# Gated layer: when the rooms in U's place are given out, and where the output's weights load

## The chip, the cores and the metric

The kernel runs on one core of one Trainium2 chip. The metric is the device time in microseconds (us) of one execution. The engines are called as in the profile: PE is TensorE (matmuls; PEld its weight loads), DVE is VectorE, ACT is ScalarE, POOL is GpSimd, and SP is SyncE, which here issues all DMAs. Each engine executes its own instructions strictly in the order of the program.

## The reference, cut to what matters

Three layers follow one another: attention over 8 heads with a window of 128 positions, a feed-forward layer with relu, and the gated layer, which the change is about. Batch is 4, sequence 576, model width 512.

```
def _moe2_ref(x, w_in, g_ln, w_sg, b_sg, w_out):        # x: 4 x 576 x 512
    h = gelu(x @ w_in)                                  # w_in: 512 x 1024
    u, v = h[..., :512], h[..., 512:]
    v_n = (v - mean(v)) / sqrt(var(v) + 1e-6) * g_ln    # over the last dimension
    v_s = einsum('ts,bsd->btd', w_sg, v_n) + b_sg       # w_sg: 576 x 576
    return x + (u * v_s) @ w_out                        # w_out: 512 x 512
```

All of it is computed in f32 quality. On the PE every f32 operand is split into a high and a low part (suffix h and l), and each product takes three matmuls: high x high, high x low, low x high. The high part is written by ScalarE (L1149), the low part is the difference to the source, written by VectorE or GpSimd (L1152).

## The kernel before, in words

**An order made by a planner.** The program is not written in a fixed order. Generators yield `Op`s, each with an engine, an expected duration, a priority, the tokens it needs and the buffers it takes. The class `Sched` (L115 to L208) simulates the engines, always takes the operation that can start earliest (among equal starts the one with the lower priority number), and lets its generator emit the instructions. So the planner's own estimates decide the order of the instructions on every engine. On the chip only that order and the semaphores count. For a load (an Op with a size, L197 to L199) it assumes 1100 ns until the transfer starts, 300 bytes per ns one transfer after another, and 1600 ns until its readers may start. Operations of the gated layer have priorities from 1000 up, except V's and U's weights and batch 0's x, which have 940 to 980.

**The gated layer** is `Phase2` (from L985). Its units of work run on the PE in this order (L992 to L994): V of batch 0, U of batch 0, Vt (V of the last 64 tokens of all four batches, taken together), V and U of batches 1, 2, 3, Ut (U of those last tokens), then S of batch 0 and 1 (the spatial product of w_sg and v), O 0 and 1 (the output of two groups of 256 tokens), S 2, O 2, O 3, S 3, O 4 to O 8. Each of V, U and S works on four quadrants with seven products of blocks instead of eight (`CHAIN`, L979), and so needs seven blocks of each operand: some are quadrants, some sums or differences of quadrants. Blocks of x are called bX, of the normalised v bN, of gated values bG. The seven products of a unit go to three PSUM banks. Product 1 is evicted by ScalarE (`evac`, L1397, into a tile te) before the third product of the chain may use its bank again; sums are made by VectorE (L1403), then GELU by ScalarE (L1420), or for S the gate (L1603, L1610).

**Rooms.** SBUF of the gated layer is handed out as numbered rooms of a kind ("X", "V", "Y", "te", "tt"). A room's entry carries the token that says from when the planner thinks it free. Rooms of kind V hold u, v, the three blocks of the last tokens' x, and gated blocks. The blocks of batch 1's and 3's v go to rooms of kind Y: three rooms of the pool p2c, and six that are cut out of the place of U's weights (tiles "more", L1375 to L1382). Those six are given out when the planner emits the fourth kind of product (P == 4, the chain's last) of U of batch 3. The tile framework makes the first write to a "more" tile wait on the chip for every matmul that still reads U's weights. Ut, which comes next on the PE, reads them too (L1501). `prep_v(1)` (L1273) begins the blocks of batch 1's v when that same product of U is done.

**Loads.** The weights of the output (wo: four pieces of 512 KB, `f64`, L1118) may load once `open_4` has run at the end of the feed-forward layer (token "room", "late"). There are two staging tiles (st), so two of them load at once and the third follows when the first piece has been worked on: ScalarE takes an absolute value (L84), VectorE does four bit operations (L89 to L96), then the split follows. The last tokens' x is loaded by `load_tail` (L1279), batch 1's x by `load_x` (L1258) in two loads; the planner plans the latter at the end of the first product of U of batch 0, and SP issues them in that order without waiting for it. All of them go through SP's one queue.

Of the kernel before, what the change touches and what calls it, by code (L numbers as in the profile page):

```python
# [8 lines left out]
F32R = mybir.dt.float32r  # L9
# [9 lines left out]
B, H, S, D = 4, 8, 576, 64  # L19
# [16 lines left out]
HOP, HOPD, HOPP = 160, 127, 280  # L36
# [78 lines left out]
class Sched:  # L115
# [49 lines left out]
    def run(self, until):  # L165
        while until not in self.done:
            best = None
            for n, p in enumerate(self.procs):
                t = self.ready(p)
                if t is None:  # L170
                    continue
                op = p[2]
                if op.alt:
                    op.eng, op.dur = min(op.alt, key=lambda z: self.at(z[0], t, z[3:]) + sum(z[1:3]))[:2]
                    op.port = op.eng == "DVE" and len(max(op.alt, key=len)) > 3
                start = self.at(op.eng, t, op.port) if op.eng else t
                key = (start + TRADE * min(max(op.pri, -99), 99), op.pri, n)
                if best is None or key < best[0]:
                    best = key, p
            assert best, [(p[2].eng, p[2].token, [x for x in p[2].need if x not in self.done], p[2].slots)  # L180
                          for p in self.procs][:40]
            (_, _, _), p = best
            op = p[2]
            t = self.ready(p)
            start = self.at(op.eng, t, op.port) if op.eng else t
            for name, bufs, tok in op.slots:
                self.slots[name].append(tok)
            for kind, n, tok in op.take:
                for _, z in self.free_of(kind)[:n]:
                    self.stock[kind][z][2] = tok  # L190
                    op.got.append(self.stock[kind][z])
            end = start + op.dur
            if op.eng:
                self.free[op.eng] = end
            if op.eng == "POOL" or op.port:
                self.port = end
            if op.size:  # L197
                self.dma = max(self.dma, start + 1100) + op.size / 300
                end = self.dma + 1600  # L199
            elif op.eng:  # L200
                end += {"DVE": HOPD, "PE": HOPP}.get(op.eng, HOP)
            if op.token:
                self.done[op.token] = end
            p[1] = start + op.dur if op.size else end
            self.now = start
            self.advance(p)
            if op.eng == "PE" and p[2] is not None and p[2].eng == "PE":
                p[1] = start + op.dur  # L208
# [771 lines left out]
TERMS = (0, 0), (0, 1), (1, 0)  # L980
MM = 113.4
DVE2 = 100


class Phase2:  # L985
# [131 lines left out]

    def f64(self, w, src, kc):  # L1118
        pri = self.wpri(w) + kc
        nd = [("room", "late")] if w == "wo" else []  # L1120
        yield Op("SP", 500, pri, need=nd, slots=[("st2", 2, ("st2", w, kc))], token=("ld2", w, kc), size=2 ** 19)
        s = self.sp.tile([128, 512], I64, tag="st", name="st", bufs=2)
        self.nc.sync.dma_start(out=s, in_=src[kc])
        ahead = [("mt", "wu", 1)] if w == "wo" else [("mt", w, 0)] if kc % 2 else [("mt", "wv", 1)] if w == "wu" else []
        yield Op("ACT", 565, pri, need=[("ld2", w, kc)] + ahead, slots=[("sc2", 3, ("sc2", w, kc))])
        j = Split64(self.nc, self.sp, 3, s)
        j.first()
        for k, z in enumerate(((0, 1), (2,), (3,))):
            yield Op("DVE", 602 if k else 680, pri, port=True, token=("st2", w, kc) if k == 2 else None)
            for n in z:  # L1130
                j.bits(n)
        self.f[w, kc] = j.x
        if w != "wo":
            yield Op(None, 0, pri, token=("f", w, kc))
            return
        yield from self.split(self.wo[0][:, kc], self.wo[1][:, kc], j.x, 512, pri)
        self.sched.done["sc2", w, kc] = self.sched.done["wo", kc] = self.sched.free[self.last] + HOP
# [5 lines left out]
    def split(self, h, l, src, w, pri, take=(), need=(), make=None, both=True):  # L1143
# [5 lines left out]
        self.nc.scalar.activation(out=h, in_=src, func=ACTF.Copy)  # L1149
        o = Op(None, 0, pri, alt=[("POOL", 150 + 2.15 * w, 0)] + [("DVE", 64 + 1.05 * w, DVE2, 1)] * both)  # L1150
        yield o
# [3 lines left out]
    def add(self, out, x, y, op, w, pri, take=(), need=()):  # L1155
        o = Op(None, 0, pri, alt=[("POOL", 150 + 2.15 * w, 0), ("DVE", 64 + 1.05 * w, DVE2, 1)], take=take, need=need)
        yield o
        if o.got:
            out = out(o.got)
        self.by(o).tensor_tensor(out=out, in0=x, in1=y, op=op)  # L1160
        self.last = o.eng
        return out
# [170 lines left out]
    def unit(self, kind, b):  # L1333
        S, n = self.sched, self.place[kind, b]
        banks, te = {}, {}
        if kind == "U":
            self.go(self.room([(("u", 2 * b + j), self.u) for j in range(2)], self.pri(kind, b), [128, 4, 256], self.start(kind, b)))
        elif kind == "V":
            self.go(self.room([((b, j), self.v) for j in range(2)], self.pri(kind, b), [128, 2, DG], self.start(kind, b)))
        after = {6: ("e", n, 1), 7: ("e", n, 6), 3: ("e", n, 5), 4: ("a", n, 7)}  # L1340
        for k, (P, bk) in enumerate(CHAIN):
            a, c = PA[P], PB[P]
            nd = self.start(kind, b) if k == 0 else [after[P]] if P in after else []
            w = {"U": "wu", "V": "wv", "S": "ws"}[kind]
            wn, key = (c, ("N", b)) if kind == "S" else (a, ("X", b))
            nd += [("w", w, wn, e) for e in range(2)] + [("b", key, a if kind == "S" else c)]
            dur = 12 * MM
            tail = kind == "S" and P in (2, 3, 7, 4)
            if tail:
                dur += 4 * MM  # L1350
                nd += [("vt", b), "kt"]
            o = Op("PE", dur, self.pri(kind, b, k), need=nd, take=[] if bk in banks else [("bank", 1, ("bk", n, bk))],
                   token=("P", kind, b, P))
            yield o
            fresh = bk not in banks
            if fresh:
                banks[bk] = self.get(o.got[0], [128, 2, 256], F32, "ps" + kind)
            ps = banks[bk]
            self.product(kind, b, ps, P, fresh)
            if tail:  # L1360
                self.rest(b, ps, P)
            if kind == "U":
                self.used(("blk", ("X", b), c), 1, "PE")
            elif kind == "S":
                self.used(("blk", ("N", b), a), 2 if a in (0, 1, 2, 3) else 1, "PE")
            if P in (1, 6, 5):
                self.go(self.evac(kind, b, n, P, ps, te))
            elif P != 4:
                i, j = {2: (0, 0), 7: (1, 1), 3: (0, 1)}[P]
                self.go(self.sum(kind, b, n, P, i, j, ps, te, bk))  # L1370
            else:
                self.go(self.use(kind, b, n, 1, 0, ps, ("bk", n, "X"), "X"))
            if P == 7:
                self.went(kind, b)
            if P == 4 and (kind, b) == ("U", B - 1):  # L1375
                for z in "hl":
                    t = self.pu.tile([128, 3584], F32R, tag="wu" + z, name="more", bufs=1)
                    for k in range(3):
                        q = S.stock.setdefault("Y", [])
                        tok = ("stock", "Y%d" % len(q))  # L1380
                        S.done[tok] = S.free["PE"] + HOPP
                        q.append([None, t[:, 48 + 1024 * k:48 + 1024 * k + 1024].rearrange("p (a b c) -> p a b c", a=2, b=2), tok])  # L1382
            if P == 5 and kind == "S":
                yield from self.narrow(b, n)

# [101 lines left out]
    def u_tail(self):  # L1487
        key, pri = ("X", B), self.pri("Ut", 0)
        self.go(self.room([(("u", G - 1), self.u)], pri, [128, 4, 256], self.start("Ut", 0)))
        for i, pairs in enumerate((((0, 0), (1, 1)), ((3, 0), (2, 2)))):  # L1490
            nd = [("w", "wu", n, e) for n, _ in pairs for e in range(2)] + [("b", key, n) for n in range(3)]
# [14 lines left out]
                self.went("Ut", 0)  # L1506
        for n in range(3):
            self.used(("blk", key, n), 1, "PE")

    def tail_u(self, i, ps, pri):  # L1510
        yield Op("ACT", 565, pri, need=[("P", "Ut", 0, i), ("ua", G - 1)], token=("bk", "Ut", i))
# [81 lines left out]
    def gate(self, b, i, j, src, tok, bank, nd, pri):  # L1593
# [11 lines left out]
        if bank:  # L1605
            S.done[tok] = S.free["DVE"] + HOP
            tok = ("gf", b)
        o = Op(None, 0, pri, alt=[("POOL", 150 + 2.15 * 512, 0), ("DVE", 602, DVE2, 1)], need=[("ur", g)])
        yield o
# [5 lines left out]
    def tail_gate(self, b):  # L1615
# [14 lines left out]
        c = slice(64 * b, 64 * b + 64)  # L1630
        o = Op(None, 0, pri, alt=[("POOL", 700, 0), ("DVE", 335, DVE2, 1)], need=[("ur", G - 1)])
        yield o
# [126 lines left out]
```

## Time and profile before

| | |
|---|---|
| median of 3 runs | 737.56 us (736.23 to 739.38) |
| the profiled execution's own time | 737.08 us |
| its span, first to last instruction | 735.3 us |
| mean granted TensorE clock | 0.990 |
| PE busy | 707.6 us, 96% |
| DVE, ACT, POOL busy | 524.8, 342.0, 194.0 us |
| DMA | 63.36 MB, mean 86 GB/s |

The profile is of one execution; times in its rows count from the start of the span. The feed-forward layer ends near 515 us, Ut near 613 us, the last output near 735 us. A busy PE in the profile is one that has matmuls in flight. In a timeline, the bracket at the end of a row gives the idle time of the engine just before it and what ended that wait.

### The profile page before, as it was taken

What the parts mean: (1) busy time and instruction counts of PE and PEld (TensorE: products, weight loads), DVE (VectorE), ACT (ScalarE), POOL (GpSimd) and SP (SyncE); (2) the same over time, 40 slices, a digit from 0 to 9 for tenths busy, and PEclk for the clock granted to TensorE, in tenths of its full rate; (3) what the DMA queues carried; (4) which work ended last, traced back from release to release, by engine and by line L of the source; (5) the groups of instructions that cost most, each with busy time, mean ns of one, the idle gap of its engine ahead of it and who ended that gap; (6) DMA issues with size and microseconds to landing.
All of it is one profiled execution on the core that took longest, in us unless ns stands there. A gap on an engine that the chain in (4) does not pass through costs nothing.

```text
span 735.3 us, 17050 instructions
## 1 busy us (share of the span) xinstructions
PE 707.6 (96%) x6734; PEld 678.0 (92%) x6734; DVE 524.8 (71%) x1396; ACT 342.0 (47%) x873; POOL 194.0 (26%) x257
## 2 busy tenths in 40 slices
PE   6889999999999999999999999999999997999997
PEld 3569999999999999999999999999899996999997
DVE  6999989899772764754753748767689867989451
ACT  5887664544532522423323524324587865534110
POOL 1455250333511411313212312001254220232010
PEclk8999999999999999999999999999999999999999
DMA  8564532033221111112032231230522100021433
GB/s 304 166 214 135 175 114 72 28 94 94 76 87 29 56 51 41 32 59 58 20 87 52 66 115 52 86 115 2 207 76 93 41 27 29 29 72 45 144 115 87
DMA packets 49423, 63.36 MB, mean 86 GB/s; under 512 B 9536, under 2 KB 37312, under 8 KB 49344
## 3 DMA queue, kind: packets, MB, share of 16 engines
q1 hardware_dynamic: 49344, 62.28, 27.0%
q8 instruction: 53, 0.87, 0.5%
q14 instruction: 26, 0.21, 0.1%
HBM read 52.83 MB, written 9.44 MB: 85 GB/s over the span
## 4 chain that ended last, share of the span: by engine, by line
PE 77%; DVE 10%; ACT 7%; DMA 3%; issue 2%; SPq 0%; POOL 0%; ACTq 0%; DVEq 0%; POOLq 0%
PE ps_h L889 26%; PE acc L900 25%; PE psO L1660 7%; PE psS L1321 5%; PE s L475 2%; PE o L660 1%; ACT t L526 1%; PE tps L616 1%; DMA st<-in_w 1%; DVE te L1403 1%; PE o L616 1%; DVE bX L1152 1%; DMA xf<-x2d 1%; PE psS L1330 1%; DVE bs L1436 1%
## 5 line engine op out<-in xcount | busy, mean ns | idle before, releaser
L831 DVE SCALAR_TENSOR_TENSOR hl<-ps_h,hh 128x512 fp32r<-128x512 f32 x72 | 49.7, 690 | 81.0 <-ACT hh L829 80.4
L829 ACT ACTIVATE hh<-ps_h 128x512 fp32r<-128x512 f32 x72 | 43.0, 597 | 119.2 <-PE ps_h L889 118.8
L900 PE MATMUL acc<-hh,w2h 128*128 128x256 f32 x576 | 92.5, 283 | 0.0
L889 PE MATMUL ps_h<-xh,w1h 128*128 128x256 f32 x576 | 91.9, 282 | 0.0
L889 PE MATMUL ps_h<-xh,w1l 128*128 128x256 f32 x576 | 90.0, 278 | 0.0
L889 PE MATMUL ps_h<-xl,w1h 128*128 128x256 f32 x576 | 90.0, 278 | 0.0
L900 PE MATMUL acc<-hh,w2l 128*128 128x256 f32 x576 | 89.9, 278 | 0.0
L900 PE MATMUL acc<-hl,w2h 128*128 128x256 f32 x576 | 89.8, 278 | 0.0
L889 PEld LDWEIGHTS ps_h<-xh,w1h 128*128 128x128 f32 x576 | 77.5, 189 | 1.4 <-issue 1.2
L900 PEld LDWEIGHTS acc<-hh,w2h 128*128 128x128 f32 x576 | 77.2, 189 | 0.1
L900 PEld LDWEIGHTS acc<-hh,w2l 128*128 128x128 f32 x576 | 77.1, 188 | 0.0
L889 PEld LDWEIGHTS ps_h<-xh,w1l 128*128 128x128 f32 x576 | 77.1, 188 | 0.0
L889 PEld LDWEIGHTS ps_h<-xl,w1h 128*128 128x128 f32 x576 | 77.0, 188 | 0.0
L900 PEld LDWEIGHTS acc<-hl,w2h 128*128 128x128 f32 x576 | 76.9, 188 | 0.0
L484 POOL TENSOR_SCALAR_AFFINE_SELECT m<-m 128x256 f32<-128x256 f32 (+1 forms) x88 | 42.0, 483 | 124.7 <-ACT m L565 123.1
L526 ACT ACTIVATE t<-t,sm 128x128 f32<-128x128 f32 x144 | 56.1, 392 | 23.5 <-DVE sm L520 22.7
L534 POOL TENSOR_TENSOR t<-t,sm 128x256 f32<-128x256 f32 x47 | 29.7, 633 | 72.3 <-DVE sm L530 52.6
L1660 PE MATMUL psO<-bG,woh 128*128 128x256 f32 x256 | 45.4, 281 | 0.0
L1321 PE MATMUL psU<-bX,wuh 128*128 128x256 f32 x224 | 40.3, 282 | 4.0 <-ACT te L1397 3.3
L1321 PE MATMUL psV<-wvh,bX 128*128 128x256 f32 x224 | 40.5, 279 | 1.9 <-ACT te L1397 1.8
L1660 PEld LDWEIGHTS psO<-bG,woh 128*128 128x128 f32 x256 | 39.1, 188 | 0.0
L1321 PEld LDWEIGHTS psU<-bX,wuh 128*128 128x128 f32 x224 | 34.2, 189 | 5.0 <-ACT te L1397 4.1
(259 smaller groups left out, 1652.5 us busy)
## 6 DMA issues: line engine op xcount, KB each, us to landing
st<-in_w SPq DMA_DIRECT2D x24, 512.0 KB, 4.3
x2d<-x SPq DMA_DIRECT2D x18, 256.0 KB, 2.0
xf<-x2d SPq DMA_DIRECT2D x9, 512.0 KB, 5.2
xr<-x2d SPq DMA_DIRECT2D x9, 512.0 KB, 4.3
st<-in_w SPq DMA_DIRECT2D x16, 256.0 KB, 2.6
st<-in_wi SPq DMA_DIRECT2D x8, 512.0 KB, 3.6
out<-xr SPq DMA_DIRECT2D x16, 256.0 KB, 2.5
rq<-in_q SPq DMA_DIRECT2D x28, 128.0 KB, 3.0
```

What stands on the lines that cost most here:

```text
L475: pe.matmul(s.S[h][hs[z], u, c0:c1], q, k, start=True, stop=True, skip_group_check=True)
L484: pool.affine_select(out=out, in_=in_, pattern=pat, compare_op=ALU.is_ge, fill=0.0, base=-1 if up else 0, channel_multiplier=1 if up else -1)
L526: act.activation(out=t[:, h], in_=t[:, h], func=ACTF.Exp, bias=st[:, h:h + 1], scale=-1.0, accum_out=sums[:, h, 0:1])
L534: pool.tensor_tensor(out=t, in0=t, op=ALU.mult, in1=st[:, 6:8].rearrange("p (h o) -> p h o", o=1).to_broadcast([128, 2, 128]))
L616: pe.transpose(spot(e)[:, h], e.t[:, h], ident)
L660: pe.matmul(pair[g][64 * h:64 * h + 64, oc:oc + w], v, s.M[m][k, h, mc:mc + w], start=x == 0, stop=x == len(mm[g]) - 1, skip_group_check=True)
L829: act.activation(out=h, in_=ps, func=ACTF.Relu)
L831: dve.scalar_tensor_tensor(out=l, in0=ps, scalar=0.0, in1=h.bitcast(F32), op0=ALU.max, op1=ALU.subtract)
L889: pe.matmul(ps[:, half], w[:, kc, f], m[:, kc], start=kc == 0 and x == 0, stop=kc == 3 and x == 2)
L900: pe.matmul(accs[half][:, d], w[:, f, ds], m[:, k], start=fi and d == 0 and k == 0 and x == 0, stop=la and k == 1 and x == 2, skip_group_c ...
L1321: pe.matmul(ps[:, e], l[s][:, kt, 128 * e:128 * e + 128], r[m][:, kt], start=fresh and e == 0 and kt == 0 and s == m, stop=kt == 1 and s = ...
L1660: nc.tensor.matmul(ps[:, e], self.wo[s][:, kc, ds], r, start=e == kc == 0 and s == m, stop=kc == 3 and s == 1, skip_group_check=True)
```

## The change

It has three parts. The six rooms in the place of U's weights are given out at the end of `u_tail`, after Ut's matmuls are planned, and no longer in `unit` after U of batch 3. The loads of the output's weights need one more token, ("xl", 1, 1): the planner's time at which the second load of batch 1's x has landed. And the planner assumes 3100 ns in place of 1600 between the transfer and the readers of a load whose priority is 1000 or more.

```
@@ Sched.run
             if op.size:
                 self.dma = max(self.dma, start + 1100) + op.size / 300
-                end = self.dma + 1600
+                end = self.dma + (1600 if op.pri < 1000 else LATE2)
@@
+LATE2 = 3100
@@ Phase2.f64
-        nd = [("room", "late")] if w == "wo" else []
+        nd = [("room", "late"), ("xl", 1, 1)] if w == "wo" else []
@@ Phase2.unit
             if P == 7:
                 self.went(kind, b)
-            if P == 4 and (kind, b) == ("U", B - 1):
-                for z in "hl":
-                    t = self.pu.tile([128, 3584], F32R, tag="wu" + z, name="more", bufs=1)
-                    for k in range(3):
-                        q = S.stock.setdefault("Y", [])
-                        tok = ("stock", "Y%d" % len(q))
-                        S.done[tok] = S.free["PE"] + HOPP
-                        q.append([None, t[:, 48 + 1024 * k:48 + 1024 * k + 1024].rearrange("p (a b c) -> p a b c", a=2, b=2), tok])
@@ Phase2.u_tail, at its end
         for n in range(3):
             self.used(("blk", key, n), 1, "PE")
+        S = self.sched
+        for z in "hl":
+            t = self.pu.tile([128, 3584], F32R, tag="wu" + z, name="more", bufs=1)
+            for k in range(3):
+                q = S.stock.setdefault("Y", [])
+                tok = ("stock", "Y%d" % len(q))
+                S.done[tok] = S.free["PE"] + HOPP
+                q.append([None, t[:, 48 + 1024 * k:48 + 1024 * k + 1024].rearrange("p (a b c) -> p a b c", a=2, b=2), tok])
```

## Rows read from the trace of the kernel before

**Rows 1.** The page: busy time, share of the span and instructions of each engine
```profile
PE 707.6 (96%) x6734; PEld 678.0 (92%) x6734; DVE 524.8 (71%) x1396; ACT 342.0 (47%) x873; POOL 194.0 (26%) x257
```

**Rows 2.** Busy time by stretch: us, PE, PEld, DVE, ACT, POOL, PEclk, DMA share, GB/s
```profile
515.00:613.00 98.00, 92.10 (x777) 90.38 (x776) 74.92 (x149) 66.75 (x120) 30.19 (x27) 1.00 0.26 89
535.00:575.00 40.00, 37.05 (x314) 36.40 (x313) 33.61 (x66) 32.10 (x56) 16.09 (x14) 1.00 0.24 77
613.00:650.00 37.00, 31.58 (x256) 31.18 (x256) 32.98 (x58) 21.78 (x40) 9.43 (x7) 0.95 0.04 15
620.00:625.00 5.00, 2.96 (x14) 2.97 (x15) 4.92 (x10) 3.54 (x7) 0.00 (x0) 0.70 0.00 0
650.00:676.00 26.00, 26.00 (x224) 26.00 (x223) 23.52 (x49) 11.01 (x20) 5.99 (x7) 1.00 0.24 82
```

**Rows 3.** PE timeline, matmuls after a wait: start, us, line, output<-inputs [idle before, releaser]
```profile
529.82 0.51 PE L1321 MATMUL psU<-bX,wuh 128*128 128x256 f32 x2 [1.55 <-ACT te L1397]
...
533.13 0.50 PE L1321 MATMUL psU<-bX,wuh 128*128 128x256 f32 x2 [0.30 <-ACT te L1397]
...
616.61 0.50 PE L1321 MATMUL psS<-wvh,bN 128*128 128x256 f32 x2 [1.90 <-DVE bN L1152]
...
622.04 0.58 PE L1321 MATMUL psS<-wvh,bN 128*128 128x256 f32 x1 [3.52 <-ACT te L1397]
```

**Rows 4.** ACT timeline, 607 to 622 us
```profile
607.62 0.61 ACT L1149 ACTIVATE bN<-v 128x512 fp32r<-128x512 f32 x1
613.03 0.63 ACT L1149 ACTIVATE more<-v 128x512 fp32r<-128x512 f32 x1 [4.80 <-PE psUt L1501]
...
614.61 0.61 ACT L1149 ACTIVATE wvh<-mx 128x512 fp32r<-128x512 f32 x1
...
618.33 1.13 ACT L1420 ACTIVATE v<-te 128x512 f32<-128x512 f32 x2
...
621.40 0.58 ACT L1397 ACTIVATE te<-psS 128x512 f32<-128x512 f32 x1
```

**Rows 5.** DVE timeline, 615 to 617 us
```profile
615.26 0.69 DVE L1152 TENSOR_TENSOR wvl<-mx,wvh 128x512 fp32r<-128x512 f32 x1 [5.41 <-ACT wvh L1149]
615.87 1.29 DVE L1152 TENSOR_TENSOR bN<-v,bN 128x512 fp32r<-128x512 f32 x2
```

**Rows 6.** Timeline of SP's DMA issues, 519 to 522 us
```profile
519.54 0.90 SPq L1123 DMA_DIRECT2D st<-in_wo  x2
520.82 0.33 SPq L1286 DMA_DIRECT2D xf<-x2d  x1
521.24 1.04 SPq L1267 DMA_DIRECT2D xf<-x2d  x2
```

**Rows 7.** ACT and DVE timelines, 525 to 530 us
```profile
525.42 0.68 ACT L84 ACTIVATE sc<-st 128x512 f32<-128x512 f32 x1 [1.24 <-DMA st<-in_wo]
526.64 0.68 ACT L84 ACTIVATE sc<-st 128x512 f32<-128x512 f32 x1 [0.54 <-DMA st<-in_wo]
...
529.19 0.58 ACT L1397 ACTIVATE te<-psU 128x512 f32<-128x512 f32 x1
...
526.94 0.68 DVE L1403 TENSOR_TENSOR te<-te,psV 128x512 f32<-128x512 f32 x1
```

**Rows 8.** POOL and PE timelines: batch 1's last block, first use of its blocks, first output
```profile
629.92 1.28 POOL L1152 TENSOR_TENSOR more<-tt,more 128x512 fp32r<-128x512 f32 x1 [14.89 <-ACT more L1149]
...
636.43 0.28 PE L1321 MATMUL psS<-wvh,more 128*128 128x256 f32 x1
...
649.76 0.40 PE L1660 MATMUL psO<-bG,woh 128*128 128x256 f32 x2
```

**Rows 9.** DVE, POOL and PE timelines: batch 1's first blocks and first matmul
```profile
534.78 1.78 DVE L1152 TENSOR_TENSOR bX<-xf,bX 128x512 fp32r<-128x512 f32 x1
...
534.68 1.34 POOL L1152 TENSOR_TENSOR bX<-xf,bX 128x512 fp32r<-128x512 f32 x1 [0.63 <-ACT bX L1149]
...
543.10 0.28 PE L1321 MATMUL psV<-wvh,bX 128*128 128x256 f32 x1
```

## The prediction

> **What bounds the kernel now.** First the page's busy line: the PE, TensorE, is busy for 96% of the span, and apart from its own weight loads nothing comes near it [rows 1]. So time is lost only where the PE stands still or runs at the low clock, and the next view is busy time by stage. From 515 us on, which is all that the change can touch, the PE is idle for 98.00 - 92.10 = 5.9 us before 613 us and for 37.00 - 31.58 = 5.4 us in 613 to 650 us; from 650 to 676 us it has no gap at all [rows 2], and the wait that ends at 622.04 us is the last that its timeline shows [rows 3]. Whatever reaches 650 us earlier should therefore end earlier by the same amount.
>
> The PE's own timeline names the gaps. Two waits of 1.55 and 0.30 us stand in batch 0's U, and two of 1.90 and 3.52 us in S of batch 0, the spatial product [rows 3]. The last is followed by matmuls at the low one of the clock's two levels, 1.2 and not 2.4 GHz: the granted clock of 620 to 625 us, part of it at each level, is 0.70, and 14 matmuls took 2.96 us, 0.211 us each, against 92.10 / 777 = 0.119 us each before [rows 2]. That is 14 x 0.092 = 1.3 us more.
>
> ScalarE's timeline shows what lies behind the pair at 613 us [rows 4]. At 607.6 us it finishes a block of V and then waits 4.80 us for the matmuls of Ut, the last tokens' U. The waiting instruction is the first that writes a tile called "more", which is U's weights given out as rooms, and Ut still reads those weights. An engine works in order, so blocks of batch 0's V and the weights of the spatial product stand behind it, though nothing they read is late. VectorE shows the echo: idle 5.41 us for a high part from ScalarE, and only then the low part of the block that S's second product needs [rows 5]. The third product waits until 622.04 us for the eviction at 621.40 us, which in ScalarE's order comes after six GELUs that begin at 618.33 us.
>
> At 520 us the same pattern appears with DMAs. SP issues two loads of the output's weights at 519.54 us, before the last tokens' x and batch 1's x [rows 6]. ScalarE then waits 1.24 and 0.54 us for these two to land, while VectorE's sum for V of batch 0 starts only at 526.94 us and the eviction that U of batch 0 waits for at 529.19 us [rows 7].
>
> **The change, part by part.**
>
> *Rooms given out after Ut.* No instruction is added or removed. The planner, which fixes every engine's order, now learns of the six rooms at Ut's end, not when batch 3's U is done, so it can no longer put a "more" write ahead of it on ScalarE. I expect ScalarE to do the blocks behind that write between 608 and 613 us. The six GELUs cannot move ahead: as I read the rooms, their results go into three that the last tokens' three x blocks hold until Ut is done, at 613.03 us. From there the six and the eviction take what they took before, 618.33 to 621.40 + 0.58 = 3.65 us, so the eviction ends near 616.7 us. S's first product ended at 616.61 - 1.90 = 614.71 us, its second took 622.04 - 3.52 - 616.61 = 1.91 us and now follows at once, to 616.6 us. The third then starts at about 616.75 us in place of 622.04: **5.3 us**. With 0.1 us of idle time left there I take the clock to stay up, as the 1.90 us gap was followed by matmuls at full rate [rows 3]: **1.3 us** more.
>
> What it costs: six of the seven blocks of batch 1's V come later in the order. Their cover is wide. The last was done at 629.92 + 1.28 = 631.2 us, and the first matmul on one of the six began at 636.43 us [rows 8]. On the chip they could not be written before 613 us in the old order either. Between nothing and the whole 1.3 us by which the PE gains more than VectorE's 5.41 us of hole, I take 0.3 us, near nothing, because of those 5.2 us: **-0.3 us**.
>
> *Output's weights behind batch 1's x.* Two issues of 512 KB move past three loads of x on SP, which waits for nothing new there: x lands earlier, and the order of SP alone does it. ScalarE's reads of the two move behind the planned landing of x. So the two waits go, and with them the late sum and eviction: **1.85 us**, both gaps of U. What is late next is their processing: three ScalarE instructions of at most 0.68 us [rows 7] for the two pieces, and one piece's work on VectorE, go into 535 to 575 us, where ScalarE is busy for 32.10 and VectorE for 33.61 of 40 us, and the PE's gaps of 40.00 - 37.05 = 2.95 us already wait mostly for ScalarE's evictions. The cost lies between nothing (free time holds it) and 3 x 0.68 = 2.0 us (each delays an eviction); I take the middle, **-1.0 us**. The later two loads shift too; their user, the output, starts only at 649.76 us [rows 8].
>
> *Landing estimate 3100 for 1600 ns.* It adds 1.5 us to what the planner believes of all loads of the second layer with these priorities, and only moves readers in the order. Nearest to an edge is batch 1's x: its first blocks were done at 536.0 and 536.6 us, its first matmul was at 543.10 us [rows 9]; less 1.5 and 1.85 us, 3.2 us of cover stay. I cost it at nothing; if that cover fails, at most 1.5 us.
>
> *Sum:* 5.3 + 1.3 - 0.3 + 1.85 - 1.0 = 7.15 us. The profiled execution took 737.08 us, 0.48 below the median of 737.56, so **729.9 us**.
>
> **The rivals.**
>
> *Only part comes (733 to 737.5 us, 19%).* A planner that is given other times makes another order from 515 us on, and the remaining gaps of 5.9 - 1.85 = 4.05 us before 613 us may grow. If the eviction of S's first product still stands behind work that was put there after Ut (six "more" high parts of 0.6 us, 3.6 us, in front of it), the first term falls to 1.7 us, and with it a 3.5 us gap and the low clock come back: 737.08 - 1.7 + 0.3 - 0.85 = 734.5 us. Against it speaks that batch 1's blocks rank behind S's evictions when both are ready.
>
> *VectorE and GpSimd block each other (732.9 us, 10%, within the ranges on either side).* A VectorE subtraction with two SBUF inputs took 1.78 us where 0.69 is usual, and it ended just after a GpSimd instruction that had begun 0.10 us before it [rows 5, 9]. So filling the hole could cost: VectorE would work without gaps beside GpSimd's 7 instructions of 613 to 650 us, and three more such meetings cost 3 x 1.1 = 3.3 us, of which the 0.3 above is part: 729.9 + 3.0. The cover of 5.2 us for batch 1's blocks speaks against it. The Trainium skill, "SBUF — State Buffer", section "SBUF: two separate sides", makes this a rule: the pair of ports that both engines share is locked for a whole instruction, and the other blocks. By that rule the row is no accident; it agrees.
>
> *Batch 1's S starves (742.1 us, 7%): slower.* Its blocks rank behind batch 0's gate. If VectorE takes S's work first, all of batch 1's, four sums and seven low parts of 0.69 us, 7.6 us, and about 3.3 us of gating stand between S of batch 0 and S of batch 1: 10.9 us of new PE wait. It decides from 7.15 us on, when it has eaten the whole sum. 729.9 + 10.9 = 740.8, and with the 1.3 us of clock that the long wait in S cost 742.1 us. Against it: S's products come one by one, and VectorE has time for the blocks between them.
>
> *The move of the loads does nothing.* The loads could run side by side, whatever their order on SP; then the waits of 1.85 us stay and the move costs no 1.0: 730.75 us, inside the forecast's range.
>
> **How the numbers follow.** Forecast as worked out, 728 to 733 us: 60%. More, 724 to 728 us, if some of the other 4.05 us of gaps goes too: 10%. Part of it: 19%. Starving: 7%. Between, 737.5 to 741 us, no gain in S and new waits before 613 us: 4%. The range of **726 to 737 us** holds the first, half of the second, most of the third. A difference of 0.5%, 3.7 us, is about what a measurement of this kernel can tell from none. Below 733.9 us lie the first two and 5 of the 19: 75% faster; 18% the same; 7% slower.
>
> **What would show it.** After: no ScalarE wait for psUt ahead of S, VectorE's 5.41 us hole gone, the third product of S within 0.5 us of the second's end, a granted clock of 1.00 throughout 613 to 650 us, and no gap after it. At 520 us: SP issues three x loads ahead of the output's weights, x lands about 2 us sooner, and the two gaps in batch 0's U are gone, with up to 1 us more in 535 to 575 us. A ScalarE eviction still late by more than 2 us in S, or a PE wait for "more" blocks at the start of batch 1's S, would make it wrong.

## The result, and the profile after

The changed kernel takes **730.34 us** (median of 4, 730.00 to 731.42) against 737.79 us for the kernel before on the same chip (4 runs): a ratio of **0.9901**, 95% interval 0.9878 to 0.9925. The profiled execution took 730.48 us with a span of 728.6; the forecast, made against a profiled execution of 737.08 us, was 729.9. The time came out. Whether the reasons did is another matter, and most of what follows is about that.

Below is the page's busy line and the busy time by stretch of the changed kernel; columns as in [rows 1, 2].

```profile
PE 706.5 (97%) x6734; PEld 676.6 (93%) x6734; DVE 529.1 (73%) x1397; ACT 342.9 (47%) x873; POOL 195.2 (27%) x256
```

```profile
515.00:613.00 98.00, 94.41 (x793) 92.73 (x792) 81.15 (x154) 70.32 (x128) 29.06 (x26) 1.00 0.28 89
613.00:650.00 37.00, 34.58 (x293) 33.99 (x292) 36.71 (x65) 19.37 (x35) 11.62 (x8) 1.00 0.05 15
620.00:625.00 5.00, 5.00 (x45) 5.00 (x44) 4.94 (x9) 3.88 (x7) 2.11 (x2) 1.00 0.35 108
650.00:676.00 26.00, 26.00 (x224) 26.00 (x223) 23.80 (x47) 11.70 (x21) 8.21 (x8) 1.00 0.31 99
```

Against [rows 2] the PE is busy for 2.3 us more before 613 us and for 3.0 us more in 613 to 650 us, the low clock of 620 to 625 us is gone (1.00 for 0.70), and VectorE works almost without a gap in 613 to 650 us (36.71 of 37 us for 32.98). The PE timeline shows which waits changed:

```profile
531.90 0.38 PE L1322 MATMUL psU<-bX,wuh 128*128 128x256 f32 x1 [1.41 <-ACT te L1390]
...
535.47 0.39 PE L1322 MATMUL psU<-bX,wuh 128*128 128x256 f32 x1 [0.39 <-DVE te L1396]
...
612.17 0.38 PE L1322 MATMUL psS<-wvh,bN 128*128 128x256 f32 x1 [0.49 <-DVE bN L1153]
...
615.01 0.38 PE L1322 MATMUL psS<-wvh,bN 128*128 128x256 f32 x1 [0.97 <-ACT te L1390]
...
641.09 0.39 PE L1322 MATMUL psS<-wvh,more 128*128 128x256 f32 x1 [1.17 <-DVE te L1396]
...
643.08 0.28 PE L1661 MATMUL psO<-bG,woh 128*128 128x256 f32 x1
```

The pair at S of batch 0 fell from 1.90 and 3.52 us [rows 3] to 0.49 and 0.97. The pair in batch 0's U, 1.55 and 0.30 us before, is still there with 1.41 and 0.39. A new wait of 1.17 us stands in S of batch 1. One measure serves all kernels below: the **stretch** from the first matmul of V of batch 0 to the first of the output. What lies ahead of it is not touched by the change and scatters between profiled executions (V began between 514.05 and 516.39 us in the 14 traces, at 515.75 before and 515.20 after), and what lies behind it took 85.5 us both before and after (735.3 - 649.76 and 728.6 - 643.08). S of batch 0 began at 612.95 us before and at 609.92 after.

| | before | after |
|---|---|---|
| V of batch 0 to S of batch 0 | 97.20 us | 94.72 us |
| S of batch 0 to the output | 36.81 us | 33.16 us |
| the stretch | 134.01 us | 127.88 us |

So 6.13 us came from the stretch: 3.65 behind S's start, and 2.48 ahead of it. The second number is a surprise, because the two gaps of U that the forecast had there did not go. SP's issues say why:

```profile
519.01 0.90 SPq L1124 DMA_DIRECT2D st<-in_wo  x2
520.48 0.33 SPq L1287 DMA_DIRECT2D xf<-x2d  x1
520.89 0.99 SPq L1268 DMA_DIRECT2D xf<-x2d  x2
```

This is the order of [rows 6]: **the loads were not moved.** The code explains it. The token ("xl", 1, 1) exists already: the feed-forward layer gives the same name to the low part of its normalised x (L756), long before `open_4` runs. `load_x` uses the name again (L1265), so a need of it is met from the start. What the name was taken to mean in the description of the change above, the landing of batch 1's second load, holds only from the third piece of the output's weights on, which is planned after `load_x` has written the name anew.

On ScalarE the wait for psUt is gone. The six GELUs and the eviction that S's third product needs now run ahead of batch 1's "more" blocks:

```profile
611.29 1.14 ACT L1413 ACTIVATE v<-te 128x512 f32<-128x512 f32 x2
612.34 1.14 ACT L1413 ACTIVATE u<-te 128x512 f32<-128x512 f32 x2
613.38 0.58 ACT L1413 ACTIVATE u<-psU 128x512 f32<-128x512 f32 x1
613.86 0.62 ACT L1413 ACTIVATE u<-te 128x512 f32<-128x512 f32 x1
614.38 0.58 ACT L1390 ACTIVATE te<-psS 128x512 f32<-128x512 f32 x1
...
616.22 1.14 ACT L1150 ACTIVATE more<-v 128x512 fp32r<-128x512 f32 x2
```

### The profile page after: what moved, and what is told of

It is laid out like the page before. It is cut to its first block, busy times and chain, and to the rows that moved or that the text cites. A ratio compares the mean times of both kernels' runs of the same rounds, so it can differ in the third digit from the quotient of the medians.

```text
span 728.6 us, 17059 instructions
## 1 busy us (share of the span) xinstructions
PE 706.5 (97%) x6734; PEld 676.6 (93%) x6734; DVE 529.1 (73%) x1397; ACT 342.9 (47%) x873; POOL 195.2 (27%) x256
## 4 chain that ended last, share of the span: by engine, by line
PE 75%; DVE 13%; ACT 5%; issue 2%; DMA 2%; POOL 1%; SPq 0%; ACTq 0%; DVEq 0%; POOLq 0%
PE acc L900 25%; PE ps_h L889 25%; PE psO L1661 7%; PE psS L1322 3%; PE s L475 2%; PE psV L1322 2%; PE o L660 1%; PE tps L616 1%; DVE tt L1161 1%; ACT t L526 1%; DVE te L1396 1%; PE o L616 1%; DMA xf<-x2d 1%; PE psU L1322 1%; DVE bX L1153 1%
```

## The experiments

Line numbers are those of the changed kernel. Ratios are to the kernel before, run on the same chip each time.

**Each part alone.** The change has three parts, so they were taken apart first.

Rooms alone:

```
-LATE2 = 3100
+LATE2 = 1600
-        nd = [("room", "late"), ("xl", 1, 1)] if w == "wo" else []
+        nd = [("room", "late")] if w == "wo" else []
```

> Only the rooms are given out after Ut; the landing estimate and the needs of the loads are as before. Theory (the parts act in different stretches and add): nothing changes before 600 us, ScalarE's 4.80 us wait for psUt goes, and of the changed kernel's gain only that of S comes: 4.0 us up to the third product of S, 1.3 us of clock, less 0 to 1.65 us of new waits in batch 1's S, so 3.7 to 5.3 us and a time of 732.5 to 734.1 us. Rival (the gain is a lucky order that needs all parts together): within 1 us of the kernel before, 737 to 738 us.

Measured: 733.46 us, ratio 0.9953 (0.9935 to 0.9971), in the theory's range. V to S took 97.24 us, as before; S to the output 33.50 instead of 36.81. The 2.48 us ahead of S is therefore not the rooms' doing. Of the two waits at the start of S of batch 0, 0.58 us is left, but three waits of 0.67, 0.53 and 1.71 us came up behind it, 2.9 us where at most 1.65 were expected.

The landing estimate alone (the kernel before with `LATE2 = 3100`):

> Only the landing estimate of 3100 ns; rooms and needs as before. Theory: ScalarE still waits some 4.8 us for psUt, the 1.90 and 3.52 us waits of S and the low clock stay, and only the 2.5 us before 613 us are gained: 735.3 us, 734.5 to 736.5. Rival: the estimate alone also moves the writes to the rooms behind Ut, and the time is that of the changed kernel, 730 to 731 us.

Measured: 745.21 us, ratio 1.0118 (1.0096 to 1.0140). S of batch 0 waited 7.93 us for its first block, and the granted clock of 613 to 650 us fell to 0.86. ScalarE's wait for psUt grew to 8.12 us. Both expectations failed, by 8 us and more.

The changed kernel without the need of ("xl", 1, 1):

```
-        nd = [("room", "late"), ("xl", 1, 1)] if w == "wo" else []
+        nd = [("room", "late")] if w == "wo" else []
```

> The changed kernel without the loads' need of the token xl 1 1. Theory: the token is an old one of the feed-forward layer, so the first two loads of the output's weights stand ahead of batch 1's x with it and without it, and only the third load's place in the plan can differ: 730.3 us within 1.5 us. Rival: the need is what gained the 2.5 us before 613 us: 732.8 us.

Measured: 741.42 us, ratio 1.0055 (1.0034 to 1.0077). Both expectations failed: the need whose first effect is nothing is worth 11 us.

The loads really moved, by a token that nobody else uses:

```
-        nd = [("room", "late"), ("xl", 1, 1)] if w == "wo" else []
+        nd = [("room", "late"), ("xload", 1, 1)] if w == "wo" else []
...
-token=("xl", b, j), size=2 ** 19)
+token=("xload", b, j), size=2 ** 19)
...
-        yield from self.prep(key, v, 2, pri, [("xl", b, 0), ("xl", b, 1)])
+        yield from self.prep(key, v, 2, pri, [("xload", b, 0), ("xload", b, 1)])
```

> The changed kernel with a token of its own for the landing of batch 1's x, so that the two loads really stand behind batch 1's x on SP. Theory of the prediction: batch 1's x lands about 2 us sooner, the gaps of 1.41 and 0.39 us in batch 0's U go, up to 1.0 us comes back between 535 and 575 us: 728.5 to 729.5 us. Rival (the gaps wait for ScalarE's evictions behind other work, not for these loads): 730.3 us within 1 us, with the gaps still there though x lands sooner.

Measured: 745.13 us, ratio 1.0108 (1.0085 to 1.0132). SP now issued the x loads first, and still a gap of 1.81 us stayed in batch 0's U; three waits of 3.61, 3.60 and 3.03 us came in S of batch 0. The theory failed by 16 us, the rival by about 14.

The last three kernels, all slower, had one thing in common on the PE: Ut was split, with its first half ahead of the last products of batch 3's U. The second set tested that, and the other factors of the table.

> Both parts as the change means them, but with the old landing estimate of 1600: the output's weights wait for a token of their own, given by batch 1's x, so that the loads do move; rooms as in the change. Its planned order of TensorE again puts the first half of Ut ahead of the last two products of batch 3's U. Theory (that split is what cost the time in the run with a true move): 738 to 743 us, waits of together over 4 us in S of batch 0. Rival (the larger landing estimate spoils the order, not the split): 731 to 734 us, no wait above 1.5 us in S of batch 0. The two waits in batch 0's U are about 1.8 us together by both, since the true move left them.

Measured: **730.20 us**, ratio 0.9904 (0.9879 to 0.9928), with Ut split as well. So the split does no harm here, and the true move with the old estimate gives what the change gives. The rival comes nearer, but is not met in full: the time lies below its range, one wait of 1.64 us is left in S of batch 0, and the two waits in batch 0's U, which both theories kept, are gone. The stretch is the shortest of all, 126.08 us. Busy time by stretch shows no gap in batch 0's U, and SP's rows, in the second fence, the order that was meant:

```profile
515.00:535.00 20.00, 20.00 (x174) 19.95 (x173) 13.78 (x28) 11.06 (x19) 4.38 (x4) 1.00 0.49 173
```

```profile
520.68 0.33 SPq L1287 DMA_DIRECT2D xf<-x2d  x1
521.11 0.85 SPq L1268 DMA_DIRECT2D xf<-x2d  x2
522.01 1.38 SPq L1124 DMA_DIRECT2D st<-in_wo  x2
```

The split undone in two of the slower kernels, by one more need on Ut's first half:

```
-need=nd + (self.start("Ut", 0) if i == 0 else [])
+need=nd + (self.start("Ut", 0) + [("P", "U", B - 1, 4)] if i == 0 else [])
```

> The kernel without the need on batch 1's x (741.4 us), and Ut made to wait in the plan for the last product of batch 3's U, so that Ut is not split. Theory (the split makes VectorE's sum of U, and behind it batch 0's V adds and the spatial weights, late): the 4.9 us wait ahead of S goes, 731 to 735 us. Rival (the late fourth load of the output's weights and what stands behind it on SP is what makes S late): at least 739 us, a wait above 3 us ahead of S or in it.

> The true move of the loads with rooms and estimate 3100 (745.1 us), and Ut unsplit in the plan in the same way. Theory (the split cost S of batch 0 its waits of 3.6, 3.6 and 3.0 us): 734 to 738 us, the granted clock of 613 to 650 us back above 0.95. Rival (moving the loads itself makes the spatial weights and batch 0's blocks late): 742 to 746 us.

Measured: 750.80 us (ratio 1.0179, 1.0152 to 1.0206) and 746.83 us (1.0140, 1.0110 to 1.0169), with waits of 7.13 and 7.66 us at S of batch 0. The theory of the split fell in both; the first rival is met, the second's 742 to 746 us was passed by 0.8.

The planning part without the rooms (the kernel before with `LATE2 = 3100` and the need):

> The change without its rooms part: landing estimate 3100 and the need of the output's weights on the token that is there already, rooms given out when batch 3's U is done. Theory (the two parts add: the change 0.9901, rooms alone 0.9953): ratio 0.9948, 732.5 to 734.5 us, with a ScalarE wait for psUt of 2 to 5 us and a wait above 2 us in S of batch 0. Rival (the planning part gains nothing by itself, the order of the change is a lucky one of both parts): 736 us or more.

Measured: 732.00 us, ratio 0.9928 (0.9904 to 0.9952). With the rooms given out as before, ScalarE still waits 3.78 us for psUt and S's second product 1.90 us (the theory asked for above 2); yet the gain is larger than that of the rooms alone. Its stretch is 129.36 us: 4.65 us from this part, 3.27 from the rooms alone, 6.13 from both, less than the sum, so the parts do not add as the theory has it. V to S took 94.85 us there: the 2.48 us ahead of S come from this part, and from estimate and need together, since with the estimate alone V to S took 106.17 us and with the rooms and the estimate but no need 103.28 us.

**What the slower kernels share.** Not the PE's order but one row sets them apart. The four pieces of the output's weights pass through two staging tiles. VectorE's last bit operation on a piece (L96) frees its tile, and k, the narrow part of the spatial weights, loads elsewhere but takes both staging tiles for its split (kh, L1150). So k waits for the fourth piece; the spatial weights stand behind k in the same generator (`w_late`), and S needs them. Below, the kernel without the need: SP's fourth issue, VectorE's last unpacking, ScalarE's split of k, and the PE's wait.

```profile
568.19 0.33 SPq L1124 DMA_DIRECT2D st<-in_wo  x1
```

```profile
590.51 0.94 DVE L96 SCALAR_TENSOR_TENSOR sc<-st,sc 128x512 int32<-128x512 int32 x1
```

```profile
595.06 0.62 ACT L1150 ACTIVATE kh<-k 128x512 fp32r<-128x512 f32 x1
```

```profile
618.84 0.58 PE L1322 MATMUL psS<-wvh,bN 128*128 128x256 f32 x1 [4.91 <-ACT bN L1150]
```

In the changed kernel the same rows are:

```profile
550.08 0.33 SPq L1124 DMA_DIRECT2D st<-in_wo  x1
```

```profile
569.90 0.69 DVE L96 SCALAR_TENSOR_TENSOR sc<-st,sc 128x512 int32<-128x512 int32 x1
```

```profile
577.76 0.62 ACT L1150 ACTIVATE kh<-k 128x512 fp32r<-128x512 f32 x1
```

A table of all (times in us, read from the same rows of each trace; the last four are still to come):

| kernel | ratio | stretch | last unpacking | k's split |
|---|---|---|---|---|
| before | 1 | 134.01 | 570.60 | 576.75 |
| changed | 0.9901 | 127.88 | 569.90 | 577.76 |
| rooms alone | 0.9953 | 130.74 | 568.95 | 575.10 |
| no rooms | 0.9928 | 129.36 | 570.14 | 578.08 |
| true move, estimate 1600 | 0.9904 | 126.08 | 575.77 | 581.53 |
| estimate 3100 alone | 1.0118 | 142.33 | 590.01 | 594.56 |
| no need | 1.0055 | 139.14 | 590.51 | 595.06 |
| true move, estimate 3100 | 1.0108 | 143.50 | 586.55 | 593.78 |
| no need, Ut whole | 1.0179 | 147.11 | 591.34 | 595.89 |
| true move, Ut whole | 1.0140 | 144.58 | 585.68 | 592.91 |
| no need, weights earlier | 0.9941 | 130.50 | 570.65 | 580.15 |
| changed, fourth load late | 1.0008 | 135.58 | 586.34 | 593.64 |
| true move, 1600, earlier | 0.9888 | 126.81 | 573.62 | 579.78 |
| changed, one add on VectorE | one run | 126.74 | 568.60 | 576.54 |

Every kernel that unpacked the last piece by 576 us gained on the kernel before; every one that did so after 585 us gained nothing or lost. A table like this is no proof, so the last set moved the last piece in both directions.

In the slower kernel without the need, the priority of the output's weights raised:

```
-"wo": self.pri("S", 0, -60)
+"wo": self.pri("U", 2, -60)
```

> The kernel without the need on batch 1's x (741.4 us, last of the four pieces of output's weights unpacked by VectorE at 590.5 us, k's high part at 595.1 us), and the priority of the output's weights raised from that of batch 0's S to that of batch 2's U. Ut is still split in the plan. Theory (k takes the staging room of the last two pieces, and behind k the spatial weights: a late last piece makes S late): last unpacking before 577 us, k's high part before 585 us, no wait above 2 us at S of batch 0, 729 to 734 us. Rival (the landing estimate spoils the order in another place): 738 us or more.

Measured: 733.83 us, ratio 0.9941 (0.9924 to 0.9957) for 1.0055; last unpacking at 570.65 us, k's split at 580.15, no wait above 0.74 us in S of batch 0. Met. But this edit raises more than the last piece: the second and third pieces are done earlier too (544.70 and 548.19 us, both near 568 us without it), and k's own priority is taken from the same number (L1522). The next run moves the fourth piece by itself.

In the changed kernel, the fourth load alone held back:

```
-        nd = [("room", "late"), ("xl", 1, 1)] if w == "wo" else []
+        nd = [("room", "late"), ("xl", 1, 1)] + [("P", "V", 2, 2)] * (kc == 3) if w == "wo" else []
```

> The changed kernel (730.3 us, fourth load of output's weights issued at 550.08 us, last unpacking at 569.9 us) with one thing added: the fourth load may be planned only behind the third product of batch 2's V. Theory (late last piece, late k, late spatial weights): fourth load at 565 us or later, last unpacking after 585 us, a wait of 3 us or more at S of batch 0, 739 to 743 us. Rival (the fourth load has cover, since the output begins only at 643 us): 729 to 733 us.

Measured: 738.91 us, ratio 1.0008 (0.9995 to 1.0021) for 0.9901, a hair under the range that was expected, as its load at 564.45 us was under the 565. The first three pieces are unpacked as in the changed kernel (529.43, 549.88 and 566.59 us, there 528.91, 549.37 and 566.07); only the fourth is late, and the rival's 729 to 733 us is out. The rows are the last unpacking, k's split, the last split of the spatial weights (wvh) ahead of S, the block bN right behind it on ScalarE, and the PE's wait for that block:

```profile
586.34 0.69 DVE L96 SCALAR_TENSOR_TENSOR sc<-st,sc 128x512 int32<-128x512 int32 x1
```

```profile
593.64 0.62 ACT L1150 ACTIVATE kh<-k 128x512 fp32r<-128x512 f32 x1
```

```profile
614.82 0.62 ACT L1150 ACTIVATE wvh<-mx 128x512 fp32r<-128x512 f32 x1
615.34 0.62 ACT L1150 ACTIVATE bN<-v 128x512 fp32r<-128x512 f32 x1
```

```profile
616.01 0.58 PE L1322 MATMUL psS<-wvh,bN 128*128 128x256 f32 x1 [4.91 <-ACT bN L1150]
```

In the changed kernel the spatial weights were split at 600.44 to 605.18 us but for one block, here mostly at 609.86 to 614.82. The planner split Ut here too, which did no harm in the true move with estimate 1600. That kernel also shows that the time of the load is not what counts: its fourth load went out at 564.71 us, as late as here, but the piece was unpacked at 575.77 us, and no wait above 0.3 us stands in the first 10 us of its S.

The best kernel with the weights earlier still:

> The best so far (both parts with the landing estimate of 1600, 730.2 us) with the priority of the output's weights raised to that of batch 2's U, so that the last piece, unpacked at 575.8 us there, comes earlier. Theory (k and the spatial weights already have cover there: no wait at S): 729 to 731.5 us, no gain beyond 0.2%. Rival (an earlier k takes load off VectorE ahead of S): 726 to 728.5 us.

Measured: 729.99 us, ratio 0.9888 (0.9868 to 0.9907). Met: the interval overlaps that of the kernel it was made from (0.9904, 0.9879 to 0.9928). Once k has cover, more cover brings nothing that can be told.

**The new wait at 641 us.** In the changed kernel VectorE's low part bG took 1.68 us, where 0.68 is usual, beside a GpSimd sum that began 0.54 us before it; the sum te that the PE waits for stands behind it. VectorE's rows, then GpSimd's:

```profile
638.76 1.68 DVE L1153 TENSOR_TENSOR bG<-te,bG 128x512 fp32r<-128x512 f32 x1
640.37 0.67 DVE L1396 TENSOR_TENSOR te<-te,psS 128x512 f32<-128x512 f32 x1
```

```profile
638.22 1.68 POOL L1161 TENSOR_TENSOR tt<-v,tt 128x512 f32<-128x512 f32 x1 [8.16 <-DVE bN L1153]
```

The test left the plan as it was and gave that one sum to VectorE when it was written out:

```
-        self.by(o).tensor_tensor(out=out, in0=x, in1=y, op=op)
+        (on or self.by(o)).tensor_tensor(out=out, in0=x, in1=y, op=op)
...
+on=self.nc.vector if (key, n) == (("N", 2), 5) else None
```

> The changed kernel, with one sum of batch 2's V (tt<-v,tt, 1.68 us on GpSimd from 638.22 us) issued on VectorE in its place, all else in the same order. Theory (GpSimd held up VectorE's bG<-te,bG, 1.68 us in place of 0.68, and through it TensorE at 641.09 us for 1.17 us): bG<-te,bG takes 0.7 us, the wait shrinks to 0.1 to 0.4 us, O of batch 0 starts 0.7 to 1.0 us sooner. Rival (that VectorE instruction waits for ScalarE or is slow of itself): its 1.68 us and the 1.17 us wait stay within 0.2 us.

```profile
637.46 0.69 DVE L1153 TENSOR_TENSOR bG<-te,bG 128x512 fp32r<-128x512 f32 x1
638.07 0.68 DVE L1396 TENSOR_TENSOR te<-te,psS 128x512 f32<-128x512 f32 x1
638.66 0.69 DVE L1161 TENSOR_TENSOR tt<-v,tt 128x512 f32<-128x512 f32 x1
```

Measured: bG at 0.69 us, no PE wait above 0.25 us left in S of batch 1, and a stretch of 126.74 us, 1.14 less than the changed kernel (0.7 to 1.0 was expected). The one execution took 728.17 us, the least seen of any kernel here, but half of its 2.3 us below the changed kernel's profiled one lies ahead of the stretch (V began at 514.05 us for 515.20, with the same instructions before it). The gain is shown by the rows, not by the time.

## Why the prediction was right in its time and half right in its reasons

**Rooms, 5.3 + 1.3 - 0.3 = 6.3 us: the mechanism right, two sizes wrong.** ScalarE's wait for psUt went, VectorE's hole of 5.41 us went, the third product followed the second after 0.97 us (the sign asked for 0.5), the clock stayed at 1.00. From S's start to its third product it was 622.04 - 612.95 = 9.09 us, now 615.01 - 609.92 = 5.09: 4.0 us for the 5.3 forecast, the first term mis-sized. The GELUs did not go back to back with Ut's end: they began at 611.29 us, 1.4 us after S did, because splits of S's own operands stood ahead of them on ScalarE. The **-0.3 us** for batch 1's blocks, taken "near nothing, because of those 5.2 us" of cover, is the second: if the clock gave its 1.3 us, 4.0 + 1.3 - 3.65 = 1.65 us came back. In the changed kernel the waits of 0.28 and 1.17 us in S of batch 1 make 1.45 of it; in the kernel with rooms alone the waits behind the third product make 0.67 + 0.53 + 1.71 = 2.9. The cover of batch 1's blocks held; the longest of these waits, 1.17 and 1.71 us, were for S's own sums, late because VectorE, now without gaps, met GpSimd (with rooms alone bG took 1.67 us beside it); the others were for ScalarE's evictions. This is the second rival, met in part: one meeting of 1.0 us where it had three of 1.1. The last experiment shows the mechanism of the 1.17 us. The Trainium skill, "SBUF — State Buffer", section "SBUF: two separate sides", says that a VectorE instruction with two SBUF inputs and a GpSimd instruction that reads SBUF hold the shared ports for a whole instruction each; the rows agree, 1.68 us for bG beside GpSimd and 0.69 us when GpSimd had nothing to do there. Such a meeting was in the kernel before too (bG of 1.67 us at 645.26 us), where it ended no wait.

**Output's weights, 1.85 - 1.0 us: the step failed for this change, and holds only with the old estimate.** The forecast says that SP issues three x loads ahead of the output's weights. It did not; the token's name was taken. What it says of the move itself, "the order of SP alone does it", failed too: the true move with estimate 3100, which is the change as it was meant, has that order on SP and kept a gap of 1.81 us, as the eviction that ends it came at 531.71 us behind other work on ScalarE. With estimate 1600 it came at 530.12 us, both gaps of U went (PE busy for 20.00 of 20 us in 515 to 535 us), and of the up to 2 us of give-back in 535 to 575 us none is seen (PE busy 37.58 us there, 37.05 in [rows 2]). The rival "the move of the loads does nothing" came true in the changed kernel, but not by loads that run side by side, as it had it.

**Landing estimate, "I cost it at nothing": the step that was wrong by most.** The working looked at the readers of batch 1's x and found 3.2 us of cover. The estimate touched another load. With it alone the kernel is 1.2% slower, and with the true move it turns 0.9904 into 1.0108: about 8 and 15 us. In both, the planner puts the unpacking of the output's fourth piece 10 to 20 us later, and behind it k and the spatial weights. In the changed kernel the need, which did not move the first two loads, holds the fourth near where it was. ScalarE's order with and without the need first parts at the third piece's absolute value (544.11 us with it, 542.98 without). Behind that VectorE's last operation on the second piece, which frees the tile for the fourth load, stands at 549.37 us with the need and at 567.48 us without, and the fourth load goes out at 550.08 and 568.19 us:

```profile
549.37 0.68 DVE L96 SCALAR_TENSOR_TENSOR sc<-st,sc 128x512 int32<-128x512 int32 x1
```

```profile
567.48 0.69 DVE L96 SCALAR_TENSOR_TENSOR sc<-st,sc 128x512 int32<-128x512 int32 x1
```

So the 2.48 us ahead of S are neither of the two effects that the forecast counted there. They are smaller waits in U and V of batches 1 to 3 (0.71 and 0.43 us left, where 0.89, 1.11, 0.94, 0.36 and 0.63 stood before) in another order, which no step forecast.

**The sum.** 7.15 us were forecast; the stretch gave 6.13, and 0.55 us lay ahead of it, where the change cannot reach. A rooms term too large by 2.65 us (6.3 for the 3.65 behind S's start) and an order gain of 2.48 us where 0.85 was counted cancelled in part, and the 0.55 us, which is scatter, closed half of the rest. The range held for that reason, not because each step was sound. Of the first rival's mechanism nothing was seen: the eviction ran ahead of the "more" parts, not behind them. Nor did batch 1's S starve, the slower rival; the way to a slower kernel that was really there, 741 to 745 us, led through the landing estimate and was not among the rivals.

**What stays open.** Why the planner, given 3100 ns, lets the fourth piece slip was read from its order only, and so was the order that gave the 2.48 us. The links between k's split and S (which of the shared rooms passes the delay on) were not cut one by one. Shown is that holding the fourth piece back, with nothing else edited, makes S late; the way back was shown only with k and the other pieces moved as well.

## What to carry to other kernels

When a planner orders the engines, cost each edit of its estimates by asking which buffers pass from one late load to the next, not only whether that load's own readers have cover: here the scarce thing was two staging tiles, and the reader of the fourth piece had some 70 us to spare (unpacked at 570, output from 643 us), while the next tenant of its tile could not bear the 16 us by which it came later (k's split at 593.64 for 577.76 us). Check that a token or a semaphore that a change waits for is not already set by someone else; the order of issue in the trace shows it in three rows. And when the time comes out as forecast, take the parts apart before believing the reasons.

## What the runs showed of the hardware that was not expected

The VectorE instruction that met GpSimd lost 1.0 us (1.68 for 0.68), and moving the GpSimd instruction to VectorE, at 0.69 us, was the cheaper way even though VectorE was busy for 36.71 of 37 us in that stage: VectorE did more work there and the PE's output began 1.1 us sooner. The long waits also cost more than themselves: in the kernels with waits of 3.0 to 7.9 us in S of batch 0, the granted clock of 613 to 650 us was 0.77 to 0.91, where the kernels without such a wait had 1.00 (a wait of 1.90 us, in the kernel without the rooms, among them), and [rows 2] 0.95 with one of 3.52 us.
